# Two blocks of the first batch transposed a second time, in the rounded four-byte type, with the scaled difference added to the residual

## The chip, the cores and the metric

One core of a Trainium2 chip runs the kernel. The metric is the device time of one execution in microseconds (us), the median of several. The engines are named as in the profile: PE (TensorE matmuls), PEld (its weight loads), DVE (VectorE), ACT (ScalarE), POOL (GpSimd) and SP (SyncE, which issues the DMAs here).

## The reference

Attention with normalised queries and keys, then a block that mixes by a Fourier transform and applies a feed-forward network (FFN):

```python
q_n, k_n = rmsnorm(q, g_q), rmsnorm(k, g_k)          # 8 batches, 12 heads, 448 rows, 64 columns
attn = softmax(q_n @ k_n^T / sqrt(64));  x = attn @ v   # as (8, 448, 768)
mixed = real(fft(fft(x, axis=1), axis=2))
u = x + mixed
un = (u - mean(u)) / sqrt(var(u) + 1e-6)
out = u + maximum(un @ w_ch1, 0) @ w_ch2              # 768 -> 3072 -> 768
```

The two weights come as eight-byte doubles, so the kernel also converts them.

## The kernel before

The work goes batch by batch. For a batch, `attention(b)` runs over six pairs of heads: load, normalise (`norm_pair`, "ss" is the sum of squares, "qkn" the normalised q and k), transpose (qk, QT, KD), scores S, softmax (P, transposed as pt into T), value product av, and the result, channels on partitions, in xT. Even and odd sums of xT (eo) feed `spectral(b)`: matmuls y with the transform's matrix give Y, matmuls ab give two banks, whose second is copied to bs, and their sum and difference go into the tile smdf.

The mixed rows fall into four tiles, `token_tile(t, mirror, ...)`: t is 0 or 1 for two halves of the row indices, mirror says whether the rows are the mirrored ones; a tile's number is i4 = 2·mirror + t. For mirror 0 ACT copies the rows, reversed, from xT to xr (the last column by a second small copy where t is 0). PE transposes six blocks of 128 columns with the identity ident, three into each of two banks (x, halves 0 and 1). DVE adds half a tile of smdf to each bank and gets u and its row sums st. SP stores u to DRAM (u_dram), ACT makes un = u − mean. Later `deviation` lets ACT square un into u's place, so this step overwrites u and waits for the store of u; in batch 0 it stands behind all four tiles in the code, but the scheduler may place it earlier. In names, u0_2 is batch 0 and i4 = 2; x0_100 is batch 0, t = 1, mirror 0, half 0.

PE then transposes un into unT (ACT and DVE empty those banks), and `ffn(b)` runs 3456 matmuls h (line L992) and as many o (L1013) over all batches. The mixing and attention of batch b + 1 are woven between the FFN matmuls of batch b.

The weights are converted on the way, in batch 0: `convert` loads a piece of doubles (dbl, line L746, into one of two buffers), ACT takes two passes (mag L749, dbl L750), DVE three (L751, L755, L759), POOL one (L763), ACT makes the rounded part w (L764) and DVE the remainder (L765); SP stores the result (L793) for later batches. Converted pieces lie in streams of three buffers. Line L114 is that of a helper which records every operation; such rows are told apart by their tiles.

The order of each engine's instructions is made by a list scheduler when the program is built, from the code's order and modelled durations; it also chooses buffers. On one engine instructions run in that order. PSUM banks are named by tags; the banks of x come from the tag "either", which alternates between two.

At the start, POOL makes ident (done at about 2.1 us), and PE runs 16 warm-up matmuls with it (L1063) before the first product of the input, qk (L334).

Of the kernel before, what the change touches and what calls it, by code (L numbers as in the profile page):

```python
# [11 lines left out]
F32 = mybir.dt.float32  # L12
F32R = mybir.dt.float32r
# [3 lines left out]
ALU = mybir.AluOpType  # L17
# [73 lines left out]
def spectral_block(ctx, tc, q, k, v, g_q, g_k, w1, w2, d1, d2, out, nb=B):  # L91
    nc = tc.nc
    PSUM = bass.MemoryType.PSUM

    cpool = ctx.enter_context(tc.tile_pool(name="cpool", bufs=1))
    sb = ctx.enter_context(tc.tile_pool(name="sb", bufs=2))
# [23 lines left out]
    V, A, G = Recorded(nc.vector), Recorded(nc.scalar), Recorded(nc.gpsimd)  # L120
# [28 lines left out]
    def bank(tag, name):  # L149
        if tag == "either":  # L150
            tag = ("q", "av")[turn[0] % 2]
            turn[0] += 1
        return ps.tile([128, 512], F32, tag=tag, name=name, bufs=BANKS[tag])
# [3 lines left out]
    def slot(tag, name, dtype=F32):  # L157
        return sb.tile([128, 900], dtype, tag=tag, name=name, bufs=SLOTS[tag])
# [4 lines left out]
    def sub(o, a, b_):  # L163
        V.tensor_tensor(out=o, in0=a, in1=b_, op=ALU.subtract)

    def add(o, a, b_):
        V.tensor_tensor(out=o, in0=a, in1=b_, op=ALU.add)

    def rows_of(n):

        return [slice(a, z) for a, z in ((0, n - n % 16), (n - n % 16, n)) if a < z]
# [5 lines left out]
    G.memset(KL.bitcast(F32), 0.0)  # L177
    ident = cpool.tile([128, 128], F32, name="ident")
    make_identity(nc, ident)
    nhalf = cpool.tile([128, 16], F32, name="nhalf")  # L180
    G.memset(nhalf, -0.5)
    gains = cpool.tile([128, 2], F32, name="gains")
# [29 lines left out]
    X_BANKS = (("either", "either"), ("either", "either"))  # L212
# [388 lines left out]
    def spectral(b, xT, EO, uns):  # L601
        a_, b_, c_ = EO
        Y = {}
        for ri in range(2):
            for st in range(2):
                n = (N1, N2)[st]
                t0 = ri * NT + st * N1
                y = bank(Y_BANKS[b > 0][st], f"y{b}_{ri}_{st}")
                yc = y[:n, :NK].rearrange("t (c i) -> t c i", c=6)
                for par in range(2):  # L610
                    turned = yc[:, 2:5:2] if par == 0 else yc[:, 1:6:4]
                    for i, (o, src, cols) in enumerate((
                        (turned, a_, slice(0, 2 * NI)),
                        (turned, b_, slice(2 * NI, 4 * NI)),
                        (yc[:, 3 * par], c_, slice(4 * NI, 5 * NI)),
                    )):
                        nc.tensor.matmul(  # L617
                            o, src[:, par, t0 : t0 + n], D1[:, ri, par, cols],
                            start=i != 1, stop=i != 0,
                        )  # L620
                Yt = slot("PT", f"Y{b}_{ri}_{st}", F32R)[:n, : 2 * NK].rearrange(
                    "s (i n) -> s i n", i=2
                )
                A.copy(Yt[:, 0], y[:n, : NK])
                sub(Yt[:, 1], y[:n, : NK], Yt[:, 0])
                Y[ri, st] = Yt
                yield 1080

        def token_tile(t, mirror, sm, df):
            i4 = 2 * mirror + t  # L630
            n = LENS[i4]
            place = "h" if b == 0 else "P"
            u = slot("P", f"u{b}_{i4}")[:n, :DM]
            st = sb.tile([N1, 4], F32, tag="st", name=f"st{b}_{i4}", bufs=4)
            if mirror:
                src = xT[:, :, 226 - t : S : 2]
            else:
                xr = slot(place, f"xr{b}_{t}")[:, : NR * n].rearrange(
                    "r (p t) -> r p t", p=NR
                )  # L640
                A.copy(xr[:, :, :N2], xT[:, :, 222 + t :: -2])
                if t == 0:
                    A.copy(xr[:, :, N2:], xT[:, :, 224:225])
                src = xr
            low, high = (df, sm) if mirror else (sm, df)
            for half in range(2):
                xp = bank(X_BANKS[b > 0][half], f"x{b}_{t}{mirror}{half}")
                for i in range(3):
                    nc.tensor.transpose(  # L649
                        xp[:n, i * 128 : (i + 1) * 128], src[:, 3 * half + i], ident  # L650
                    )
                V.scalar_tensor_tensor(
                    out=u[:, half * 384 : half * 384 + 384],
                    in0=xp[:n, :384],
                    scalar=0.0,
                    in1=high[:n, 384:0:-1] if half else low[:n, :384],
                    op0=ALU.add,
                    op1=ALU.add,
                    accum_out=st[:n, half : half + 1],
                )  # L660
            for r in rows_of(n):
                nc.sync.dma_start(u_dram[b % 2, i4, r, :DM], u[r])
            V.tensor_scalar(
                out=st[:n, 2:3], in0=st[:n, 0:1], scalar1=st[:n, 1:2], scalar2=-1.0 / DM,
                op0=ALU.add, op1=ALU.mult,
            )
            un = slot(place, f"un{b}_{i4}")[:n, :DM]
            A.activation(un, u, AF.Identity, bias=st[:n, 2:3])
            uns[i4] = un
            return i4, u, un, st  # L670

        def deviation(i4, u, un, st):
            n = LENS[i4]
            A.activation(u, un, AF.Square, accum_out=st[:n, 3:4])
            rstd = sb.tile([N1, 1], F32, tag="rstd", name=f"rstd{b}_{i4}", bufs=8)
            V.tensor_scalar(
                out=st[:n, 3:4], in0=st[:n, 3:4], scalar1=1.0 / DM, scalar2=EPS,
                op0=ALU.mult, op1=ALU.add,
            )
            G.tensor_tensor(  # L680
                out=rstd[:n], in0=st[:n, 3:4], in1=nhalf[:n, :1], op=ALU.pow
            )
            rstds[b, i4] = rstd

        rest = []
        for t in range(2):
            n = (N1, N2)[t]
            ab = []
            for i in range(2):
                o = bank("S", f"ab{b}_{t}_{i}")[:n, : NK]  # L690
                c = abs(t - i)
                kk = (N1, N2)[c]
                for x_, (a, z) in enumerate(((0, 0), (0, 1), (1, 0))):
                    nc.tensor.matmul(  # L694
                        o, D2[:kk, i, t, a, :n], Y[i, c][:, z], start=x_ == 0, stop=x_ == 2
                    )
                ab.append(o)
            bs = slot("P", f"bs{b}_{t}")[:n, : NK]
            A.copy(bs, ab[1])
            sdt = slot("P", f"smdf{b}_{t}")[:n, : 2 * NK].rearrange(  # L700
                "s (i n) -> s i n", i=2
            )

            def nat(ap):
                return ap.rearrange("t (i c) -> t c i", c=6)

            def half(ap):
                return ap.rearrange("t (c i) -> t c i", c=6)

            add(nat(sdt[:, 0]), half(ab[0]), half(bs))  # L710
            sub(nat(sdt[:, 1]), half(ab[0]), half(bs))
            yield 980
            for mirror in range(2):
                made = token_tile(t, mirror, sdt[:, 0], sdt[:, 1])
                if b:
                    deviation(*made)
                else:
                    rest.append(made)
                yield 620
        for made in rest:  # L720
            deviation(*made)
# [387 lines left out]
```

## Time and profile before

| | us |
|---|---|
| median of three runs | 2168.9 (2167.07 to 2169.48) |
| span of the profiled execution | 2158.8 |
| PE busy | 2085.6 (97%) |
| DVE busy | 1551.6 (72%) |
| ACT busy | 1053.9 (49%) |
| POOL busy | 343.4 (16%) |

The span runs from the first to the last instruction that the profiler records; the run's time lies 10.1 us above it. Batch 0's attention takes the first 140 us, its mixing runs to about 177, and the first h of the FFN is at 177.06. Rows of a timeline give start, duration, engine, line, operation and tiles; in brackets stands how long the engine was idle before and what it waited for.

### The profile page before, as it was taken

The page shows a single profiled execution, that of the slowest core. Times are in us where ns is not written, and L with a number is a line of the kernel's source. Part 1 is how long each engine was busy: PE and PEld are TensorE (multiplying, and loading weights), DVE is VectorE, ACT ScalarE, POOL GpSimd, SP SyncE. Part 2 cuts the span into 40 slices and gives each one's busy share as a digit, 9 for nine tenths or more (in the row PEclk, how much of TensorE's full clock was granted, in tenths as well). Part 3 has the DMA queues.
Part 4 walks back from the last instruction along what each step waited for, and adds up shares of the span by engine and source line. Part 5 has one row for each costly group of instructions (what it writes and reads, how often), then busy time and mean ns, then how long its engine had stood idle before and what let it go on. Part 6 is the DMA issues. An engine that isn't in the chain of part 4 may idle for free.

```text
span 2158.8 us, 31384 instructions
## 1 busy us (share of the span) xinstructions
PE 2085.6 (97%) x11224; PEld 1858.1 (86%) x11224; DVE 1551.6 (72%) x3016; ACT 1053.9 (49%) x2258; POOL 343.4 (16%) x196
## 2 busy tenths in 40 slices
PE   7878999899999999999999999999999999999998
PEld 4557788788999999999999999999999989999998
DVE  7888788877885788758786688857787578754122
ACT  7967776455552555435552455425553355422100
POOL 4323334311110111001110011101110011000000
PEclk8977999999999999999999999999999999999999
DMA  5548877757555855667555666558556674458774
GB/s 172 181 125 272 257 249 255 243 200 214 170 167 182 238 180 168 175 206 225 161 176 177 215 197 176 171 190 239 171 165 188 204 209 142 150 175 251 234 248 150
DMA packets 294976, 424.79 MB, mean 197 GB/s; under 512 B 183283, under 2 KB 221156, under 8 KB 294820
## 3 DMA queue, kind: packets, MB, share of 16 engines
q1 hardware_dynamic: 290386, 420.67, 63.5%
q10 hardware_dynamic: 4434, 2.11, 0.4%
q8 instruction: 89, 1.46, 0.3%
q14 instruction: 67, 0.55, 0.1%
HBM read 362.53 MB, written 65.31 MB: 198 GB/s over the span
## 4 chain that ended last, share of the span: by engine, by line
PE 77%; DMA 3%; DVE 3%; ACT 1%; issue 1%; POOL 0%; DVEq 0%; SPq 0%; POOLq 0%; ACTq 0%
PE h L992 28%; PE o L1013 28%; PE S L382 5%; PE av L492 4%; PE pt L480 4%; DMA dbl<-w 2%; PE y L617 1%; PE qk L334 1%; PE oT L949 1%; PE x L649 1%; PE un L861 1%; PE av L497 1%; PE ab L694 1%; PE rem L437 1%; DMA u_dram<-u 1%
## 5 line engine op out<-in xcount | busy, mean ns | idle before, releaser
L1013 PE MATMUL o<-hs,w 128*128 128x448 f32 x3456 | 793.2, 372 | 2.9 <-DVE rounded L114 0.9
L992 PE MATMUL h<-unT,w 128*128 128x448 f32 x3456 | 784.0, 371 | 1.0 <-DVE hs L114 0.6
L1013 PEld LDWEIGHTS o<-hs,w 128*128 128x128 f32 x3456 | 638.4, 188 | 60.5 <-issue 3.8
L992 PEld LDWEIGHTS h<-unT,w 128*128 128x128 f32 x3456 | 639.8, 189 | 57.5 <-issue 4.1
L114 ACT ACTIVATE P<-S,mn 112x448 f32<-112x448 f32 x384 | 243.9, 637 | 196.9 <-DVE mn L114 188.1
L114 DVE TENSOR_REDUCE mn<-S 112x1 f32<-112x448 f32 x384 | 233.8, 617 | 33.0 <-PE S L382 30.3
L114 ACT ACTIVATE hs<-h 128x448 fp32r<-128x448 f32 x192 | 104.4, 544 | 304.5 <-PE h L992 302.9
L114 DVE SCALAR_TENSOR_TENSOR hs<-h,hs 128x448 fp32r<-128x448 f32 x192 | 119.3, 621 | 149.3 <-ACT hs L114 147.3
L114 DVE TENSOR_TENSOR acc<-o,acc 128x448 f32<-128x448 f32 (+1 forms) x240 | 147.0, 613 | 81.8 <-PE o L1013 79.1
L114 POOL TENSOR_TENSOR qkn<-raw 112x1024 f32<-112x1024 f32 x36 | 69.2, 1924 | 677.4 <-PE qk L334 391.5
L114 POOL TENSOR_TENSOR ss<-ss,nhalf 112x16 f32<-112x16 f32 x48 | 143.6, 2992 | 205.6 <-DVE ss L114 183.6
L382 PE MATMUL S<-KD,QT 128*112 128x448 f32 x384 | 152.8, 400 | 18.5 <-ACT KD L114 15.6
L114 ACT CAST T<-pt 128x448 fp32r<-128x448 f32 x216 | 112.9, 533 | 101.5 <-PE pt L480 97.9
L492 PE MATMUL av<-T,vhl 128*128 128x448 f32 x432 | 154.2, 385 | 0.8 <-DVE T L114 0.8
L114 DVE TENSOR_TENSOR T<-pt,T 128x448 fp32r<-128x448 f32 x216 | 131.7, 617 | 25.7 <-ACT T L114 24.7
L382 PE MATMUL S<-rounded,QT 128*112 128x448 f32 x384 | 143.7, 376 | 0.0
L114 DVE TENSOR_SCALAR P<-P,sm 112x448 f32<-112x448 f32 x288 | 122.7, 465 | 3.9
L480 PE MATMUL pt<-ident,P 112*128 112x112 f32 x864 | 122.1, 258 | 0.0
L480 PEld LDWEIGHTS pt<-ident,P 112*128 112x128 f32 x864 | 102.7, 140 | 15.8
L763 POOL TENSOR_TENSOR mag<-mag,dbl 128x512 uint32<-128x512 uint32 (+1 forms) x46 | 77.6, 1686 | 170.3 <-DVE mag L759 115.2
L114 POOL TENSOR_TENSOR rstd<-st,nhalf 112x1 f32<-112x1 f32 (+2 forms) x32 | 18.2, 570 | 505.7 <-DVE st L114 500.1
L382 PEld LDWEIGHTS S<-KD,QT 128*112 128x112 f32 x384 | 68.5, 179 | 29.4 <-ACT KD L114 18.7
(116 smaller groups left out, 2528.3 us busy)
## 6 DMA issues: line engine op xcount, KB each, us to landing
w<-w SPq DMA_DIRECT2D x192, 768.0 KB, 5.4
w<-w SPq DMA_DIRECT2D x288, 512.0 KB, 4.5
dbl<-w SPq DMA_DIRECT2D x28, 512.0 KB, 5.3
dbl<-w SPq DMA_DIRECT2D x18, 768.0 KB, 5.1
raw<-q SPq DMA_DIRECT2D x96, 112.0 KB, 3.9
raw<-k SPq DMA_DIRECT2D x96, 112.0 KB, 4.0
v<-v SPq DMA_DIRECT2D x96, 96.0 KB, 3.6
u_dram<-u SPq DMA_DIRECT2D x24, 336.0 KB, 3.1
```

The lines of the kernel that those rows point to most:

```text
L114: ins = emit(*args, **kwargs)
L334: nc.tensor.transpose(pt[:, c * C : (c + 1) * C], qk[:, i, c].rearrange("t h d -> t (h d)"), ident[:C, :C],)
L382: ins = nc.tensor.matmul(s_, QT[:, h, cs], K[:, h], start=step == 0, stop=step == 1)
L437: nc.tensor.transpose(rem[:, c * C : (c + 1) * C], Pc[c][:, 384:512], ident[:C, :C])
L480: nc.tensor.transpose(pt[:, c * C : (c + 1) * C], Pc[c][:, 512 * h + j * 128 : 512 * h + (j + 1) * 128], ident[:C, :C],)
L492: nc.tensor.matmul(av[:, :S], lv, T[:, i], start=(j == 0 and i == 0), stop=False)
L497: nc.tensor.matmul(av[:, :S], lv, R[:, h], start=False, stop=True)
L617: nc.tensor.matmul(o, src[:, par, t0 : t0 + n], D1[:, ri, par, cols], start=i != 1, stop=i != 0,)
L649: nc.tensor.transpose(xp[:n, i * 128 : (i + 1) * 128], src[:, 3 * half + i], ident)
L763: behind(nc.gpsimd.tensor_tensor(out=bits, in0=bits, in1=low, op=ALU.add))
L992: pace(nc.tensor.matmul(o, w[:, a, c], unT[c][:, z], start=n == 0, stop=n == 17))
L1013: pace(nc.tensor.matmul(o, w[:, a, f], hs[4 * g + f][:, z], start=n == 0, stop=n == 11))
```

## The change

A second identity, identr, in the rounded four-byte type F32R, is copied from ident by ACT at the start. In batch 0, for the two tiles with mirror 0, SP copies the first three blocks of xr to a tile xq of that type, PE transposes these into a bank with identr, ACT copies the bank to xc, DVE makes xc the difference of the plain transpose and xc, and DVE adds 1e6 times this difference to the half of smdf that the tile's u is made from.

```diff
     ident = cpool.tile([128, 128], F32, name="ident")
     make_identity(nc, ident)
+    identr = cpool.tile([128, 128], F32R, name="identr")
+    A.copy(identr, ident)
...
                 src = xr
+                if b == 0:
+                    xq = sb.tile([128, 384], F32R, tag="xq", name=f"xq{t}", bufs=1)
+                    nc.sync.dma_start(
+                        xq[:, :3*n].bitcast(F32), xr[:, :3].rearrange("r p t -> r (p t)")
+                    )
+                    xqp = bank(X_BANKS[b > 0][1], f"xq{b}_{t}{mirror}")
+                    for i in range(3):
+                        nc.tensor.transpose(
+                            xqp[:n, i * 128 : (i + 1) * 128].bitcast(F32R), xq[:, i*n:i*n+n], identr
+                        )
+                    xc = sb.tile([128, 384], F32, tag="xc", name=f"xc{t}", bufs=1)
+                    A.copy(xc[:n], xqp[:n, :384])
...
                         xp[:n, i * 128 : (i + 1) * 128], src[:, 3 * half + i], ident
                     )
+                if b == 0 and not mirror and not half:
+                    sub(xc[:n], xp[:n, :384], xc[:n])
+                    V.scalar_tensor_tensor(out=low[:n, :384], in0=xc[:n], scalar=1e6, in1=low[:n,:384], op0=ALU.mult, op1=ALU.add)
```

The scheduler's order changes around it. On ACT, from the copy bs of t = 1 to the first unT, before:

```order
L114 COPY bs0_1_1545<-ab0_1_1_1541 112x390
L114 ACTIVATE un0_2_1535<-u0_2_1520,st0_2_1521 111x768
L114 COPY xr0_1_1565<-xT0_295 128x672
L750 ACTIVATE dbl_0_1_1628<-dbl_0_1_1628 128x768
L114 ACTIVATE u0_0_1500,st0_0_1501<-un0_0_1518 113x768
...
L114 ACTIVATE un0_1_1579<-u0_1_1563,st0_1_1564 112x768
...
L114 ACTIVATE un0_3_1595<-u0_3_1581,st0_3_1582 112x768
L114 CAST unT0_0_1685<-un0_0_1680 128x448
```

And now (lines below the change have moved, L749 and L750 are L766 and L767 here):

```order
L114 COPY bs0_1_1557<-ab0_1_1_1553 112x390
L114 ACTIVATE u0_0_1502,st0_0_1503<-un0_0_1530 113x768
L114 ACTIVATE un0_2_1547<-u0_2_1532,st0_2_1533 111x768
L114 COPY xr0_1_1577<-xT0_297 128x672
...
L766 ACTIVATE mag_0_1_1649<-dbl_0_1_1650 128x768
L114 COPY xc1_1585<-xq0_10_1581 112x384
...
L114 ACTIVATE un0_1_1601<-u0_1_1575,st0_1_1576 112x768
...
L114 ACTIVATE un0_3_1617<-u0_3_1603,st0_3_1604 112x768
L781 CAST w1_0_2_1661<-mag_0_2_1662 128x768
L766 ACTIVATE mag_0_4_1677<-dbl_0_4_1678 128x768
L767 ACTIVATE dbl_0_4_1678<-dbl_0_4_1678 128x768
L114 CAST unT0_0_1707<-un0_0_1702 128x448
```

The Square of u0_0 has moved ahead of un0_2 and xr0_1, the copy xc1 is new behind mag_0_1, and the conversion steps of mag_0_4 now stand ahead of the first unT.

On DVE, the first tile's u and the conversion of the piece mag_0_0, before:

```order
L751 TENSOR_SCALAR mag_0_0_1614<-mag_0_0_1614 128x768
L755 TENSOR_SCALAR mag_0_0_1614<-mag_0_0_1614 128x768
L759 SCALAR_TENSOR_TENSOR mag_0_0_1614<-dbl_0_0_1615,mag_0_0_1614 128x768
L114 TENSOR_TENSOR smdf0_0_1497<-ab0_0_0_1487,bs0_0_1495 113x6x65 x2
L114 SCALAR_TENSOR_TENSOR u0_0_1500,st0_0_1501<-x0_000_1505,smdf0_0_1497 113x384
L114 SCALAR_TENSOR_TENSOR u0_0_1500,st0_0_1501<-x0_001_1510,smdf0_0_1497 113x384
```

And now:

```order
L768 TENSOR_SCALAR mag_0_0_1636<-mag_0_0_1636 128x768
L772 TENSOR_SCALAR mag_0_0_1636<-mag_0_0_1636 128x768
L114 TENSOR_TENSOR smdf0_0_1499<-ab0_0_0_1489,bs0_0_1497 113x6x65 x2
L776 SCALAR_TENSOR_TENSOR mag_0_0_1636<-dbl_0_0_1637,mag_0_0_1636 128x768
L114 SCALAR_TENSOR_TENSOR smdf0_0_1499<-xc0_1513,smdf0_0_1499 113x384
L114 SCALAR_TENSOR_TENSOR u0_0_1502,st0_0_1503<-x0_001_1522,smdf0_0_1499 113x384
L114 SCALAR_TENSOR_TENSOR u0_0_1502,st0_0_1503<-x0_000_1515,smdf0_0_1499 113x384
```

The last step of mag_0_0 has moved behind smdf, and the addition of the difference stands between it and u.

Again on DVE, the stretch around u0_1 as it is now (before, u0_1 stood directly behind the second st of tile 0, with mag_0_1 behind u0_3):

```order
L114 TENSOR_SCALAR st0_2_1533<-st0_2_1533 111x1
L768 TENSOR_SCALAR mag_0_1_1649<-mag_0_1_1649 128x768
L114 TENSOR_TENSOR xc1_1585<-x0_100_1587,xc1_1585 112x384
L772 TENSOR_SCALAR mag_0_1_1649<-mag_0_1_1649 128x768
L114 SCALAR_TENSOR_TENSOR smdf0_1_1559<-xc1_1585,smdf0_1_1559 112x384
L768 TENSOR_SCALAR mag_0_2_1662<-mag_0_2_1662 128x768
L114 SCALAR_TENSOR_TENSOR u0_1_1575,st0_1_1576<-x0_101_1594,smdf0_1_1559 112x384
L776 SCALAR_TENSOR_TENSOR mag_0_1_1649<-dbl_0_1_1650,mag_0_1_1649 128x768
L114 SCALAR_TENSOR_TENSOR u0_1_1575,st0_1_1576<-x0_100_1587,smdf0_1_1559 112x384
```

The two conversions' steps have moved ahead of and between the halves of u0_1, with the subtraction and the addition among them. On PE the three rounded transposes stand between the halves x0_000 and x0_001; x0_001 uses the bank of the rounded ones. On SP the copy to xq0 stands ahead of the load dbl_0_0, that to xq1 behind the stores of u0_2 and ahead of the load dbl_0_2, and dbl_0_1 now stands behind the two stores of u0_0. At the start, ACT's table load and the cast to identr stand ahead of the wait for the first input.

## Rows read from the trace of the kernel before

**Rows 1.** The page: busy time of each engine; the chain that ended last.

```profile
PE 2085.6 (97%) x11224; PEld 1858.1 (86%) x11224; DVE 1551.6 (72%) x3016; ACT 1053.9 (49%) x2258; POOL 343.4 (16%) x196
...
PE 77%; DMA 3%; DVE 3%; ACT 1%; issue 1%; POOL 0%; DVEq 0%; SPq 0%; POOLq 0%; ACTq 0%
```

**Rows 2.** Busy time by stretch: PE, PEld, DVE, ACT, POOL, granted clock, DMA share, GB/s.

```profile
20.00:50.00 30.00, 20.90 (x98) 14.25 (x97) 26.64 (x48) 29.61 (x64) 14.12 (x7) 0.84 0.63 197
...
160.00:178.00 18.00, 9.82 (x41) 8.26 (x42) 14.68 (x37) 13.58 (x22) 6.75 (x6) 0.50 0.70 238
```

**Rows 3.** Timeline of the start: start us, us, engine, line, operation, tiles, idle before.

```profile
2.16 9.34 PE L1063 MATMUL warmed<-warm,ident 128*128 128x512 f32 x16 [2.16 <-POOL ident masks.py:199]
...
4.75 1.28 ACT L114 ACT_TABLE_LOAD   x1 [4.75 <-DMA raw<-k]
...
6.05 1.06 ACT L114 ACTIVATE qkn<-raw 112x1024 f32<-112x1024 f32 x1
...
12.51 1.11 PE L334 MATMUL qk<-ident,qkn 112*128 112x112 f32 x8 [1.02 <-DVE qkn L114]
```

**Rows 4.** Timeline of PE where the mixing begins.

```profile
141.63 1.62 PE L649 MATMUL x<-ident,xr 128*113 128x128 f32 x6 [1.01 <-ACT xr L114]
144.82 1.21 PE L617 MATMUL y<-D,eo 128*113 128x130 f32 x4 [1.57 <-DVE eo L114]
```

**Rows 5.** Timeline of ACT from the first tile to unT.

```profile
141.39 0.18 ACT L114 COPY xr<-xT 128x6 f32<-128x6 f32 x1
...
157.57 0.46 ACT L114 COPY bs<-ab 113x390 f32<-113x390 f32 x1
...
165.17 0.79 ACT L114 COPY xr<-xT 128x672 f32<-128x672 f32 x1
...
167.24 0.84 ACT L114 ACTIVATE u<-un 113x768 f32<-113x768 f32 x1
...
171.58 0.93 ACT L114 ACTIVATE un<-u,st 112x768 f32<-112x768 f32 x1
...
175.02 0.92 ACT L114 ACTIVATE un<-u,st 112x768 f32<-112x768 f32 x1
176.47 1.84 ACT L114 CAST unT<-un 128x448 fp32r<-128x448 f32 x4 [0.54 <-PE un L861]
```

**Rows 6.** Timeline of DVE: smdf and u of the tiles, and one conversion later.

```profile
158.08 0.96 DVE L759 SCALAR_TENSOR_TENSOR mag<-dbl,mag 128x768 uint32<-128x768 uint32 x1
158.96 1.55 DVE L114 TENSOR_TENSOR smdf<-ab,bs 113x390 f32<-113x390 f32 x2
160.34 0.56 DVE L114 SCALAR_TENSOR_TENSOR u<-x,smdf 113x384 f32<-113x384 f32 x1
...
169.03 0.56 DVE L114 SCALAR_TENSOR_TENSOR u<-x,smdf 112x384 f32<-112x384 f32 x1 [0.66 <-POOL rstd L114]
...
415.30 0.56 DVE L751 TENSOR_SCALAR mag<-mag 128x768 f32<-128x768 f32 x1 [3.49 <-ACT mag L749]
```

**Rows 7.** DMA issues by tile: count, KB each, median us from issue to landing.

```profile
dbl<-w SPq DMA_DIRECT2D x18, 768.0 KB, 5.1
...
u_dram<-u SPq DMA_DIRECT2D x24, 336.0 KB, 3.1
...
v<-rounded SPq DMA_DIRECT2D x24, 16.0 KB, 2.0
```

**Rows 8.** Timelines of SP's queue and of POOL.

```profile
161.15 0.37 SPq L746 DMA_DIRECT2D dbl<-w  x1
...
174.87 2.03 POOL L763 TENSOR_TENSOR mag<-mag,dbl 128x768 uint32<-128x768 uint32 x1 [3.72 <-ACT mag L749]
```

**Rows 9.** Busy time by stretch, 186 to 426 us: the sum of eight stretches.

```profile
sum 240.00, PE 231.12 PEld 191.60 DVE 196.44 ACT 163.73 POOL 91.81; mean PE 28.89 PEld 23.95 DVE 24.56 ACT 20.47 POOL 11.48
```

**Rows 10.** Waits of PE, 178 to 500 us: total, times, longest, in us.

```profile
PE y L617 <- DVE eo L114: 4.2, 1, 4.2
```

**Rows 11.** The chain that ended last: start us, us, what.

```profile
406.94 7.35 DMA dbl<-w
```

## The prediction

> **What bounds the kernel now.** The page's first part and its chain come first [rows 1]: PE is busy 2085.6 us of a span of 2158.8 us (97%), and PE has 77% of the chain that ended last. So the change is worth what it does to the few places where PE waits. It touches two of them. The table of stretches [rows 2] shows the larger: PE is busy 9.82 of the 18 us from 160 to 178, at a granted clock of 0.50, while no engine is full (DVE 14.68, ACT 13.58). There the first batch's mixing hands over to its FFN, and a chain of single steps on DVE, ACT, SP and PE rules. The other is the first 12 us [rows 3]. In batch 0's FFN, from 186 to 426, PE is busy 231.12 of 240 us [rows 9], so 8.9 us are all that is idle there. Next the rows of PE, ACT and DVE in the handover [rows 4 to 6] give the steps' durations, and the landings of DMAs [rows 7] what a copy costs. From batch 1 on the changed kernel has its old order nearly throughout; what is decided before about 480 us is simply carried.
>
> The added work as such is small. Six transposes are 1.62 us of PE by the six that stand there now [rows 4]; two ACT copies of 384 columns cost 0.46 each by the bs row [rows 5]; four DVE operations of 0.56 each by the u row make 2.2 [rows 6]. What counts is the chain they lengthen, and the neighbours the scheduler changed.
>
> **Part 1, the start.** PE's warm-up, which reads ident, starts at 2.16; ACT's table load starts at 4.75, when the first k is there, and the Square at 6.05 [rows 3]. In the new order the table load and the cast to identr stand ahead of the wait for the input, so both run in ACT's dead time, and the Square can start when the data is there: up to 1.28 earlier, and so can ss, qkn and the first qk. But PE's warm-up matmuls run from 2.16 to 11.50, and PE waits only 1.02 more before qk at 12.51. So the gain is at most 1.0, and at least 0. I take −1.0, because ACT, which the next stretch hangs on, is busy 29.61 of 30 us from 20 to 50 [rows 2] and keeps what it is given. A page differs on the size, though not on the sum: the Trainium skill, ScalarE: Activation LUTs, What ACT_TABLE_LOAD costs, gives 1283 ns for the load and 1380 ns for a drain. The row has 1.28, and the Square 0.02 after it, so no drain shows here; with one the gain would be 2.66, and the warm-up would cap it at 1.0 as well.
>
> **Part 2, the tile t=0.** The last column of xr is written at 141.57 [rows 5]. From there: the copy to xq, which SP issues and PE now waits for. The nearest rows are v<-rounded, also from on-chip memory to on-chip memory, 16 KB in 2.0, and u_dram<-u, 336 KB in 3.1 [rows 7]; xq has 174 KB, and I take 2.6 (bounds 2.0 and 3.1). Landed 144.2; three transposes 0.8; the copy to xc 0.46, which the second half's transposes wait for, because x0_001 takes xq's bank; these 0.8. So y starts at 146.3 against 144.82 [rows 4], +1.5. On the size of the copy a page speaks: the Trainium skill, DMA: Bandwidth & Descriptors, Latency and other measured facts, says that the access to HBM is the dominant part of a DMA's fixed 2 us; this copy touches no HBM. The 2.0 row touches none either, so the row gives little sign of such a saving; by the page the copy would lie at 2.0 or under, and the sum would be about 1.2 less over the two copies.
>
> Of these 1.5 little reaches smdf: it started at 158.96 because DVE was still in the last step of mag_0_0 (158.08 for 0.96) [rows 6], and this step has been moved behind smdf. smdf stays at 159.0; then come the moved step (0.9) and the new addition (0.55). u0_0, at 160.34 before, is +1.4, and un0_0 behind it.
>
> **Part 3, the tile t=1.** Here the order changes for the worse. The Square of u0_0 now stands on ACT ahead of un0_2 and of the copy xr0_1. It overwrites u0_0, so it waits for the two stores of u0_0: end of u 162.7, plus 3.1 [rows 7], 165.8. Square 1.0 (0.84 and a read), 166.9; un0_2 0.84, 167.7; xr0_1 0.79, 168.5, against 165.96 (165.17 and 0.79) [rows 5]: +2.5. Then xq1 lands at 171.1 and is transposed at 171.9. ACT gets to its copy xc1 only behind dbl_0_1 (SP issues it behind the two u0_0 stores, at 0.4 each [rows 8], at 163.6; 5.1 to landing [rows 7], 168.7), two casts, a Square and mag_0_1: five passes of some 0.84 by the Square's row, 172.9, and 173.4 with the copy. On DVE u0_1 stands behind the subtraction, a shift, the new addition and the first step of mag_0_2. Its load is issued behind xq1, at 169.0; with 5.1 to landing and 0.9 on ACT it is there at 175.0, and 0.5 on DVE follow. So u0_1 starts at 175.5, not at 175.0 behind xc1 (173.4, and 1.6 of DVE), against 169.03 [rows 6]: +6.5.
>
> **Part 4, the last two tiles and unT.** Between u0_1 and un0_1 DVE has two halves of u, a mag step of 0.96, another of 0.55, half of u0_3 and st: 3.2, so un0_1 at 178.7, against 171.58 [rows 5] +7.1. un0_3 follows a Square that again waits for a store, and ends at 182.5 against 175.94, +6.6. PE's transposes of un are ready then, but ACT now has mag_0_4 and dbl_0_4 ahead of unT0_0: their load gets its buffer when POOL has done mag_0_1 (DVE at 177.0, POOL 2.03 [rows 8]), at 179.0, lands at 184.1, and two passes of 0.84 take 1.7. unT0_0 at 185.8 against 176.47 [rows 5], +9.3. The FFN's first matmul needs unT0_0; the later columns of unT hang on un0_3 too and not on that load alone, so they come back towards its +6.6. Between 6.6 and 9.3 I take **+8** for the start of the FFN. The low granted clock in this stretch [rows 2] is there in both, and only its end moves.
>
> **Part 5, what batch 0 gives back.** PE is idle 8.9 us from 186 to 426, and then waits 4.2 for eo ahead of y [rows 10]: 13.1 in all could swallow the delay, where what PE waited for does not itself wait for PE. The weight conversions (SP load, ACT, DVE, POOL) don't, until their three buffers are full; attention of batch 1 does, since its S and pt stand between the h. What speaks for giving back is DVE's idle 3.49 for a conversion at 415.30 [rows 6], in front of the eo that y waits for: there DVE waits for ACT and ACT for a load of 7.35 [rows 11], not for PE. I take 3.5; bounds 0 and all. The stretch is also put into another order, which I can't price.
>
> **Sum.** −1.0 + 8.0 − 3.5 = +3.5 of the span of 2158.8. The median, 2168.9, is 10.1 more than the span of the profiled execution; I add the difference to the median: **2172.4 us**. A measurement of this kernel tells about 0.2% from no change, 4.3 us: 2164.6 to 2173.2.
>
> **The rivals.**
> A, the forecast: late FFN, partly given back: +1 to +7, 2170 to 2176. Chance 0.55.
> B, all of it hidden: conversions and loads go on while PE waits, and PE catches up in its 13.1 idle us. Then −1 + 8 − 8, 2168, within −2 and +1 with the short copy. For it: the chain of work there runs over the loads and not over PE, as these two rows show; against: PE's idle is in small pieces, behind attention's own results. 0.20.
> C, faster: the idle of batch 0 goes for good, because while PE stands the conversions and batch 1's attention run ahead by as much, and no later wait comes back. −1 + 8 − 13.1 = −6.1, 2163. It decides faster by over 0.2% from 11.3 swallowed. Against it: conversions can only be three buffers ahead. 0.08.
> D, nothing given back or more added: the new order of batch 0 brings waits of its own, or ACT's waits for loads are longer than 5.1 because the DMA engines are already at 0.70 there [rows 2]. +7 to +12, 2176 to 2181, about 2178. 0.17.
> That the edit does nothing is no rival for time: its instructions stand in the order; whether the rounded transpose differs from the plain one is a value, multiplied and added either way.
>
> **How the numbers follow.** D and A's upper part lie over 2173.2: 0.17 + 0.23 = 0.40 slower; C's larger part is faster, 0.06; same 0.54. The range leaves out C and the far ends of D and B: 2167 to 2179. The likeliest case by itself has 2170 to 2176.
>
> **What would show it.** Right: the Square of qkn at about 4.8 and qk at 11.5; y at 146; u0_1 at 175 and unT0_0 at 185 with ACT waiting for dbl_0_4; less than 8.9 of PE idle in the FFN. Wrong: unT0_0 under 180 (the load or the stores land sooner, or DVE is ahead), a wait of over 5 for xq, or new waits of PE between 200 and 480.

## The result

The changed kernel takes 2177.0 us (median of five runs, 2173.8 to 2183.7) against 2168.9 for the kernel before: a ratio of 1.0054, with a 95% interval from 1.0040 to 1.0069. That is slower by more than 0.2%, and more than the +3.5 us of the forecast. A second comparison gave 1.0038 (1.0024 to 1.0053). Both say slower, by 8 to 12 us.

Runs of the kernel before spread from 2159 to 2172 us, and its profile shown ahead belongs to one of its quickest. The profiled execution of the changed kernel took 2179.3 us with a span of 2177.3, so about 2 us lie outside a span, and the 10.1 of the prediction were mostly the distance between a quick run and the median. The two spans therefore differ by more (18.5) than the kernels do, and a second profile of the kernel before (`b_again`, below, span 2164.7) is used as its partner from here on.

The page of the changed kernel: its span, the busy times, the chain that ended last.

```profile
span 2177.3 us, 31352 instructions
...
PE 2092.2 (96%) x11230; PEld 1860.8 (85%) x11230; DVE 1554.1 (71%) x3020; ACT 1056.0 (48%) x2261; POOL 340.6 (16%) x196
...
PE 78%; DMA 9%; DVE 5%; ACT 5%; issue 2%; POOL 1%; SPq 0%; DVEq 0%; POOLq 0%; ACTq 0%
```

Against [rows 1]: PE's work is nearly the same (2092.2 us busy against 2085.6). The shares of the two chains can't be set side by side: this one is followed back to the start, that of before only to 313.85 us, so its shares come to 85% of the span.

The start, in the timeline (start us, us, engine, line, operation, tiles, idle before); it answers to [rows 3]:

```profile
0.73 1.28 ACT L114 ACT_TABLE_LOAD   x1 [0.73 <-PEq L1109]
...
5.15 1.06 ACT L114 ACTIVATE qkn<-raw 112x1024 f32<-112x1024 f32 x1 [2.72 <-DMA raw<-k]
...
11.63 1.10 PE L336 MATMUL qk<-ident,qkn 112*128 112x112 f32 x8
```

The table load has moved into ACT's dead time, and qk starts 0.88 earlier. The handover to the FFN, timelines of PE, then ACT, then DVE, POOL and PE again; they answer to [rows 4 to 6]:

```profile
144.02 0.83 PE L654 MATMUL xq<-identr,xq 128*113 128x128 f32 x3 [1.14 <-DMA xq<-xr]
145.42 0.98 PE L663 MATMUL x<-ident,xr 128*113 128x128 f32 x3 [0.57 <-ACT xc L114]
146.19 1.07 PE L619 MATMUL y<-D,eo 128*113 128x130 f32 x4
...
171.45 0.56 PE L654 MATMUL xq<-identr,xq 128*112 128x128 f32 x3 [2.22 <-DMA xq<-xr]
```

```profile
165.84 0.84 ACT L114 ACTIVATE u<-un 113x768 f32<-113x768 f32 x1 [1.64 <-DMA u_dram<-u]
...
167.50 0.79 ACT L114 COPY xr<-xT 128x672 f32<-128x672 f32 x1
170.06 0.88 ACT L767 ACTIVATE dbl<-dbl 128x768 uint32<-128x768 uint32 x1 [1.77 <-DMA dbl<-w]
...
173.70 0.45 ACT L114 COPY xc<-xq 112x384 f32<-112x384 f32 x1
...
180.66 0.94 ACT L114 ACTIVATE un<-u,st 112x768 f32<-112x768 f32 x1 [4.87 <-issue]
...
183.89 0.82 ACT L781 CAST w<-mag 128x768 fp32r<-128x768 f32 x1
184.62 0.89 ACT L766 ACTIVATE mag<-dbl 128x768 f32<-128x768 f32 x1
185.41 0.90 ACT L767 ACTIVATE dbl<-dbl 128x768 uint32<-128x768 uint32 x1
186.21 1.81 ACT L114 CAST unT<-un 128x448 fp32r<-128x448 f32 x4
```

```profile
175.24 0.55 DVE L114 SCALAR_TENSOR_TENSOR smdf<-xc,smdf 112x384 f32<-112x384 f32 x1
175.71 0.55 DVE L768 TENSOR_SCALAR mag<-mag 128x768 f32<-128x768 f32 x1
176.17 0.55 DVE L114 SCALAR_TENSOR_TENSOR u<-x,smdf 112x384 f32<-112x384 f32 x1
...
178.00 1.98 DVE L772 TENSOR_SCALAR mag<-mag 128x768 uint32<-128x768 uint32 x1
```

```profile
177.74 1.83 POOL L780 TENSOR_TENSOR mag<-mag,dbl 128x768 uint32<-128x768 uint32 x1 [3.81 <-DVE mag L776]
```

```profile
186.77 0.74 PE L1009 MATMUL h<-unT,w 128*128 128x448 f32 x1 [1.72 <-ACT unT L114]
```

The steps of the prediction stand here in its order: the Square waits for the store, then xr, the load, xc, u0_1 at 176.2, un0_1 at 180.7, unT at 186.2. Two of its waits do not: DVE has no idle time from 173.83 to u0_1, so the load of mag_0_2, whose step stands ahead of it, had come by then; and ACT has none between 180.66 and unT, so it did not wait for dbl_0_4 either. The first h, at 177.06 in the profile ahead and 178.69 in `b_again`, is at 186.77. Busy times of the two stretches around it (PE, PEld, DVE, ACT, POOL, granted clock, DMA share, GB/s):

```profile
160.00:178.00 18.00, 7.03 (x27) 5.16 (x27) 12.56 (x33) 9.51 (x15) 4.54 (x5) 0.50 0.62 208
178.00:200.00 22.00, 15.49 (x75) 13.25 (x76) 19.30 (x36) 16.96 (x30) 10.11 (x7) 0.69 0.87 298
```

In the first, PE has 7.03 us of work where it had 9.82 [rows 2]. And the waits of PE from 195 to 520 (total, times, longest):

```profile
PE av L458 <- ACT T L114: 7.3, 6, 2.3
PE un L878 <- ACT un L114: 4.8, 1, 4.8
PE y L619 <- DVE eo L114: 3.5, 1, 3.5
```

The wait for eo [rows 10] has hardly shrunk, so little was given back there, and the waits for T have grown: `b_again` has 2.1 us of them in three. One of them, on PE and, just ahead of it, on ACT:

```profile
265.55 2.31 PE L458 MATMUL av<-T,v 128*128 128x448 f32 x4 [1.97 <-ACT T L114]
```

```profile
263.75 0.89 ACT L767 ACTIVATE dbl<-dbl 128x768 uint32<-128x768 uint32 x1 [2.24 <-DMA dbl<-w]
264.54 0.53 ACT L114 ACTIVATE hs<-h 128x448 fp32r<-128x448 f32 x1
264.97 0.96 ACT L114 COPY T<-pt 128x448 f32<-128x448 f32 x2
```

ACT stands in front of a conversion step whose load has not landed, with T queued behind it, and PE waits for T. It is a wait of the new order, not of the new work: `before_neworder` (below), which has the one without the other, has it too (2.01 us at 264.1).

### The profile page after: what moved, and what is told of

Same layout as the page of the kernel before. It is cut to its first block, busy times and chain, and to the rows that moved or that the text cites. A ratio compares the mean times of both kernels' runs of the same rounds, so it can differ in the third digit from the quotient of the medians.

```text
span 2177.3 us, 31352 instructions
## 1 busy us (share of the span) xinstructions
PE 2092.2 (96%) x11230; PEld 1860.8 (85%) x11230; DVE 1554.1 (71%) x3020; ACT 1056.0 (48%) x2261; POOL 340.6 (16%) x196
## 4 chain that ended last, share of the span: by engine, by line
PE 78%; DMA 9%; DVE 5%; ACT 5%; issue 2%; POOL 1%; SPq 0%; DVEq 0%; POOLq 0%; ACTq 0%
PE h L1009 28%; PE o L1030 27%; PE S L384 6%; DMA dbl<-w 5%; PE av L494 4%; PE pt L482 4%; DMA u_dram<-u 2%; PE y L619 2%; PE qk L336 1%; PE av L458 1%; POOL mag L780 1%; PE oT L966 1%; ACT P L114 1%; DMA w<-w 1%; PE rem L439 1%
## 5 line engine op out<-in xcount | busy, mean ns | idle before, releaser
L780 POOL TENSOR_TENSOR mag<-mag,dbl 128x512 uint32<-128x512 uint32 (+1 forms) x46 | 77.1, 1675 | 176.8 <-DVE mag L776 137.4
L384 PEld LDWEIGHTS S<-KD,QT 128*112 128x112 f32 x384 | 69.0, 181 | 31.3 <-ACT KD L114 19.7
```

Of the source, the lines that this page charges most:

```text
L384: ins = nc.tensor.matmul(s_, QT[:, h, cs], K[:, h], start=step == 0, stop=step == 1)
L780: behind(nc.gpsimd.tensor_tensor(out=bits, in0=bits, in1=low, op=ALU.add))
```

## The experiments

Two theories and a rival. **Handover**: what costs is the FFN's late start. **Order**: what costs is the other order of batch 0's FFN. **Work**: the copies and added steps cost it, however ordered. The scheduler mixes all three, so most kernels here hold every engine to a given order from the first instruction into batch 1's FFN, by dependencies that only fix the order of issue (PINNED lists, for each engine, the numbers of its instructions in the order to hold; the cuts further down give a list in words):

```diff
+PINNED = {
...
+    for numbers in PINNED.values():
+        row = [f"I-{n}" for n in numbers.split()]
+        for one, two in zip(row, row[1:]):
+            tc.add_manual_dep(
+                nc.get_inst_by_name(two), one,
+                mybir.DependencyInfo(mybir.DependencyClass.NoSync, mybir.DependencyReason.DATA),
+                reason="issue order",
+            )
```

"Old" is the order of the kernel before, "new" that of the changed one; the cut between handover and FFN is the last unT on each engine (on POOL the last rstd of batch 0, on SP the last store of u). The times below are ratios to the kernel before, run on the same chip; 0.001 is 2.2 us. The expectations quote differences of means, which lie within 1 us of these. That holding an order costs nothing in itself was not measured alone; `before_warm` below, held to the old order, comes to 0.9995.

| kernel | handover | FFN | added work | ratio (95%) | first h | first h to second FFN |
|---|---|---|---|---|---|---|
| b_again | old | old | no | 1 | 178.7 | 296.8 |
| before_newhandover | new | old | no | 1.0019 (1.0010, 1.0029) | 185.7 | 292.1 |
| before_newffn | old | new | no | 1.0021 (1.0010, 1.0032) | 178.0 | 301.7 |
| before_neworder | new | new | no | 1.0030 (1.0017, 1.0043) | 185.9 | 297.4 |
| after_oldorder | old | old | yes | 1.0007 (0.9994, 1.0019) | 181.6 | 298.4 |
| after_oldffn | new | old | yes | 1.0031 (1.0019, 1.0042) | 186.1 | 295.5 |
| after_oldhandover | old | new | yes | 1.0039 (1.0026, 1.0053) | 179.8 | 304.2 |
| after_again | new | new | yes | 1.0038 (1.0024, 1.0053) | 187.7 | 301.0 |

The last column is the time from the first h of batch 0 to the first of batch 1, in us, with 1392 or 1393 recorded matmuls in each. Its source for three of them and for the first profile of the changed kernel, as stretches with busy times (b_again, before_newhandover, before_newffn, after):

```profile
178.69:475.44 296.75, 279.86 (x1392) 236.19 (x1393) 235.83 (x398) 191.39 (x373) 103.38 (x63) 0.97 0.76 249
```

```profile
185.72:477.77 292.05, 276.60 (x1393) 233.40 (x1393) 231.51 (x392) 189.16 (x369) 100.34 (x61) 0.98 0.75 248
```

```profile
177.95:479.64 301.69, 280.82 (x1393) 236.26 (x1393) 239.68 (x398) 192.48 (x373) 102.16 (x64) 0.96 0.75 245
```

```profile
186.77:488.61 301.84, 281.48 (x1392) 235.68 (x1393) 233.06 (x392) 189.42 (x369) 99.93 (x61) 0.96 0.74 240
```

**b_again**: the kernel before, unchanged, for a second profile.

> The kernel before, profiled a second time. Its five times lie between 2161.9 and 2169.5, and its first profile has a span of 2158.8, which belongs to the lowest. Handover theory and order theory alike: a span of about 2159 to 2167, with the first h at 177 again. If a span near 2166 shows, the places where it differs from the first are what varies from run to run, and have to be kept out of the comparison.

One time, 2166.5, span 2164.7, the first h at 178.69. It is 1.6 later there than in the first profile and 6.0 later at the end; it serves as the partner of the profiles below.

**identr_only**: the cast to identr, nothing else; every other row keeps its place.

```diff
     make_identity(nc, ident)
+    identr = cpool.tile([128, 128], F32R, name="identr")
+    A.copy(identr, ident)
```

> Only the cast to identr at the start; every engine's order is else that of before. Term 1 of the prediction: ACT's table load at about 0.7, the first qk about 0.9 earlier, and all of it carried: -0.9 us, between -1.5 and 0. If the start is not on the path: 0.

1.0003 (0.9988 to 1.0018). The first qk is at 11.49:

```profile
11.49 1.11 PE L336 MATMUL qk<-ident,qkn 112*128 112x112 f32 x8 [0.49 <-DVE qkn L114]
```

So the start is 1.0 earlier, as predicted, but at the end a gain of 1.0 can't be told from none within this interval. Whether it is carried stays open. The trace also shows how far single profiles differ: with the order of before, its stretch from the first h to the second FFN is 4.1 shorter than that of `b_again`, and the profile ahead has 295.90. So a few us in this stretch tell little without the ratio beside them.

```profile
177.85:470.50 292.65, 276.12 (x1393) 233.84 (x1393) 235.78 (x398) 191.81 (x373) 103.51 (x63) 0.97 0.77 253
```

**after_oldorder**: the changed kernel, old order throughout.

```diff
+PINNED = the order of before, the new instructions free between
```

> The changed kernel, all its work, with every engine held to the order of before (order-only dependencies up to batch 1); the new instructions stand between. Handover theory (what is late at the start of the FFN is kept): u0_1 waits for xq1 and xc1, some 4 us later, first h at about 180 to 181 and a time of +2 to +4 us over before. Order theory (the reordering costs, the work nearly nothing): 0 to +3. Work theory (the copies over SP and the extra steps cost it all, however they are ordered): +10 to +12.

1.0007 (0.9994 to 1.0019), first h at 181.57. The work theory falls for this kernel: all the added work costs about 1.5 us when the order stays, not 8 to 12.

**before_neworder**: nothing added, new order throughout.

```diff
+PINNED = the order of the changed kernel, without its new instructions
```

> The work of before, with every engine held to the order of the changed kernel. Order theory: nearly the whole loss, +8 to +12 us, with PE waiting 5 us or more for T in the FFN as in the changed kernel. Handover theory: the Square's wait for the stores and the conversions ahead of u0_1 and unT are there, the copies to xq are not, so the first h at 183 to 185 and +6 to +8. Work theory: 0 to +2.

1.0030 (1.0017 to 1.0043): +6.5 us without one added instruction, the first h at 185.91. Most of the loss is the order. The time fits the handover theory better and the waits for T fit the order theory, so the two were cut apart.

**after_again**, the changed kernel beside the next three.

```diff
 (no edit to the changed kernel)
```

> The changed kernel once more, beside the same runs of before as the three that follow. If order and work add up from the two held kernels (+7.0 for the order, +1.6 for the work): +8 to +9. If the two make each other worse: +10 to +13 as in the first comparison. First h at 185 to 187.

1.0038, +8.2 us: what the order (+6.5) and the work (+1.5) give together.

**before_newhandover** and **before_newffn**: each half of the new order alone.

```diff
+PINNED = new up to the last unT, old from there      (before_newhandover)
+PINNED = old up to the last unT, new from there      (before_newffn)
```

> The work of before; new order only up to the last unT, the old order in the FFN and batch 1's attention. Handover theory: first h at about 186, and +6 to +8 us, as in the kernel with the new order throughout. FFN-order theory (the reordered FFN makes the loss): 0 to +2, since the late start is made up.

> The work of before; old order up to the last unT, the new order after it. Handover theory: first h at about 178, 0 within 2 us. FFN-order theory: +5 to +8 us, with PE waiting 2 us each three times for T as in the changed kernel.

1.0019 and 1.0021: each theory foresaw one of them at nothing, and both cost some 4 us. With the new handover alone the first h is 7.0 later than in `b_again`, and the stretch behind it 4.7 shorter (296.75 to 292.05), which is no more than `identr_only` differs without a late start. The ratio says it better: +4.1 at the end (2.2 to 6.3) of 7.0, so some 3 us were given back. PE's wait for eo, 4.2 to 4.3 us in `before`, `b_again` and `identr_only`, is 1.8 here. With the new FFN order alone the first h is not late at all, the stretch is 4.9 longer, and PE waits for T (from 195 to 520, in before_newffn and then in `b_again`):

```profile
PE av L466 <- ACT T L124: 5.2, 6, 2.3
```

```profile
PE av L456 <- ACT T L114: 2.1, 3, 1.4
```

In the eight kernels of the table these waits come to 5.2 to 8.4 us where the FFN order is new and to 0.5 to 2.1 where it is old.

**after_oldhandover** and **after_oldffn**: the same cut in the changed kernel.

```diff
+PINNED = old up to the last unT, its own from there  (after_oldhandover)
+PINNED = its own up to the last unT, old from there  (after_oldffn)
```

> The changed kernel with all its work; old order up to the last unT, its own order after it. Handover theory: first h at 181 to 182 and +1 to +3, as with the old order throughout. FFN-order theory: +7 to +9.

> The changed kernel with all its work; its own order up to the last unT, the old order after it. Measured so far against before: new handover order +3.8, new FFN order +4.4, both +7.1, the work in the old order +1.7, all of the change +9.1. If the FFN order is a cost of its own that a late start does not hide: +4 to +6, first h at 187. If only the late start counts: +8 to +9.

1.0039 and 1.0031. With the first, the expectation of the handover theory (+1 to +3) was missed and that of the FFN order (+7 to +9) met: with the new FFN order, a first h 7 us earlier brought nothing. With the second, +6.7 us was above what I had put (+4 to +6), within the interval. Averaged over the four pairs of the table that differ in one column alone, the new handover costs 2.8 us, the new FFN order 3.8 and the work 2.4. They don't simply add: a late first h costs 4.1 and 5.2 with the old FFN order, 2.0 and −0.2 with the new one. The mixtures also have waits of their own: PE waits 3.1 us and more for KD near 195 where old handover meets new FFN, which neither whole order has, so each figure is good to a microsecond or two.

**before_newffn_a**: only the first part of the new FFN order. It was meant to reach about 310 us; in the trace PE and ACT leave the new order for the old near 275 us and DVE near 285.

```diff
+PINNED = old, new from the last unT to about 280 us, old from there
```

> The work of before; new order only in the first half of batch 0's FFN (to about 310 us), the old order before and after it. One-place theory (the wait of PE for KD at 194, 3.3 us with a stretch of half clock behind it, is most of the loss): +3 to +4.5. Many-places theory (waits for T spread over the whole FFN): +1.5 to +2.5.

1.0003 (0.9994 to 1.0012). Both expectations missed: this part costs nothing that can be measured, although the wait for KD is in it (2.01 us at 194.6). What the new FFN order costs lies behind some 280 us or needs both parts; the second part alone was not tried. The waits for T go with the loss: 0.5 us here, and of the 5.2 in before_newffn 4.1 at 337 and 391. In the traces the kernels also part there in the pace of the conversions, POOL's step for each piece. Six pieces in a row, the first and the last of them, in before_newffn and then in before_newffn_a:

```profile
296.75 1.29 POOL L773 TENSOR_TENSOR mag<-mag,dbl 128x512 uint32<-128x512 uint32 x1 [1.24 <-ACT T L124]
...
336.32 1.79 POOL L773 TENSOR_TENSOR mag<-mag,dbl 128x512 uint32<-128x512 uint32 x1 [1.70 <-DVE mag L769]
```

```profile
298.88 1.31 POOL L773 TENSOR_TENSOR mag<-mag,dbl 128x512 uint32<-128x512 uint32 x1 [3.10 <-DVE sums L124]
...
332.65 2.35 POOL L773 TENSOR_TENSOR mag<-mag,dbl 128x512 uint32<-128x512 uint32 x1 [2.18 <-ACT P L124]
```

39.6 us for these in the new order, 33.8 in the old one. In all the kernels up to here the last of these POOL steps and the start of the second FFN move together, 25 to 27 us apart: 449.9 and 475.4 in b_again, 453.3 and 479.6 in before_newffn, 461.9 and 488.6 in the changed kernel.

**before_warm**: matmuls without use in PE's gaps of the handover, old order.

```diff
+KEPT = 34
...
+    kept = bank("ffn", "kept")
+    for _ in range(KEPT):
+        nc.tensor.matmul(kept[:, :128], ident, ident, start=True, stop=True)
+PINNED = old, 10, 8, 12 and 4 of these in the four gaps from 157 to 176
```

> Before, in its own order, with 34 matmuls of ident by ident (128 columns, results unread) in the four gaps of PE between 157 and 176. If the half clock at the start of the FFN comes from PE's idle time in the handover: granted clock over 0.8 from 178 on, the first eight h in 2 us in place of 3.3, and 1 to 4 us less in all. If the clock does not follow them: 0 within 1.5, or +1 where they overrun a gap.

0.9995 (0.9986 to 1.0005), the same. The stretches of this kernel:

```profile
160.00:178.00 18.00, 13.38 (x96) 12.02 (x95) 14.68 (x37) 13.65 (x22) 6.42 (x6) 0.88 0.69 238
178.00:200.00 22.00, 21.47 (x103) 18.15 (x102) 19.72 (x33) 16.99 (x31) 9.92 (x6) 0.86 0.84 283
```

The granted clock followed in the first stretch (0.88, it was 0.50 [rows 2]); but PE still waited 3.09 us ahead of un0_1, and the first h ran at the half clock as before (0.74 us, at a granted clock of 0.50 from 176.9 to 178.5). What filling that gap too would give stays open.

**t0_only**: the change on the tile t = 0 alone, the scheduler free.

```diff
-                if b == 0:
+                if b == 0 and t == 0:
...
-                if b == 0 and not mirror and not half:
+                if b == 0 and t == 0 and not mirror and not half:
```

> The change on tile t = 0 alone; half of the added work, and the scheduler makes an order of its own again (the Square of u0_0 ahead of un0_2 as in the changed kernel, other places in the FFN). Work theory: +0.8. Order theory: not half of the change's +9.1, but what its own order gives: the first h at 182 to 186, and +2 to +9.

1.0025 (1.0014 to 1.0036), +5.4 us for half of the work, with the first h at 178.14, no later than before. The expected late first h did not come; the loss did, in the stretch behind it (302.2 us). Its order is again another one, and PE's waits for T come to 6.2 us (195 to 520, 2.1 in `b_again`), with one of 2.9 for xT and one of 2.2 for hs beside them.

**Third buffers.** That POOL's steps move with the end could make the conversion loop the cause or a follower. The next kernels hold the order and give the loop a third buffer, for the loaded doubles (tag X, which the eo tiles share) and for the words made from them (M).

```diff
-    SLOTS = {"P": 8, "PT": 6, "M": 2, "unT": 6, "h": 6}
+    SLOTS = {"P": 8, "PT": 6, "M": 3, "unT": 6, "h": 6}
...
-        return sb.tile([128, 1800], dtype, tag="X", name=name, bufs=2)
+        return sb.tile([128, 1800], dtype, tag="X", name=name, bufs=3)
```

`before_3buf_old` is before with its own order, `before_x3_old` and `before_m3_old` have one of the two lines; `after_3buf_own` and `after_3buf_old` are the changed kernel in its own and in the old order, `after_3buf` leaves the scheduler free.

> Before, in its own order, with three buffers in place of two for the loaded doubles and for the words made from them, so that a load no longer waits for POOL's last step two pieces back. Conversion theory (the two-buffer loop of load, ACT, DVE, POOL is what batch 0's FFN keeps step with; its 60th POOL step at 447 to 450 now): that step 3 us or more earlier, and 2 to 7 us less in all. PE theory (PE, 94 to 95 per cent busy there, sets the pace): ACT's waits for loads go, but the time is the same within 1.5.

> Before, own order, a third buffer for the loaded doubles alone. Conversion theory with the load's wait as its cause: most of the -12.9, between -13 and -8. If the wait is for the other buffer (the words made from them): -3 to 0.

> Before, own order, a third buffer for the words made from the doubles alone. Conversion theory with the load's wait as its cause: -3 to 0. If the wait is for this buffer (ACT's mag pass waits until DVE's last step two pieces back): -13 to -8.

> The changed kernel in its own order with the same third buffers. Conversion theory: its 60th POOL step comes down from 462 to 455 or less, and the loss against before shrinks from +9.1 to between 0 and +5. PE theory: still +8 to +10.

> The changed kernel with the third buffers and the scheduler free to make a new order. Conversion theory: as the one before, 0 to +5, or less where the scheduler also uses the slack. Order theory alone: anything between 0 and +9, as its new order happens to fall.

> The changed kernel, all its work, in the order of before, with the third buffers. Conversion theory: what the order cost is gone and the loop has its slack: about -12 (before with third buffers: -12.9) plus 1.7 for the work in this order, so -13 to -9, faster than both kernels. If work and buffers interfere: -8 to 0.

| kernel | ratio (95%) | first h | first h to second FFN |
|---|---|---|---|
| before_3buf_old | 0.9939 (0.9927, 0.9951) | 174.6 | 286.5 |
| before_x3_old | 0.9945 (0.9931, 0.9959) | 173.9 | 286.5 |
| before_m3_old | 0.9989 (0.9980, 0.9999) | 177.7 | 294.3 |
| after_3buf_own | 1.0013 (1.0004, 1.0022) | 186.7 | 291.6 |
| after_3buf | 1.0005 (0.9996, 1.0014) | 188.1 | 289.5 |
| after_3buf_old | 0.9988 (0.9979, 0.9998) | 180.7 | 288.1 |

The loop is a cause and not a follower: with no instruction moved, a third buffer of the tag X makes the kernel before 12 us quicker (`before_x3_old`, 2151.6 us), which beats both kernels and is more than the 2 to 7 us I expected of both buffers; the buffer of the words alone gives 2.4. How much of the 12 us is the loads' and how much that of the eo tiles, which share the tag, was not separated. Its stretch from the first h to the second FFN, and its last POOL step in the timeline, at 434.6 against 449.9:

```profile
173.93:460.43 286.50, 274.37 (x1392) 231.97 (x1393) 238.73 (x398) 191.56 (x373) 104.05 (x64) 0.98 0.80 259
```

```profile
434.56 1.53 POOL L773 TENSOR_TENSOR mag<-mag,dbl 128x512 uint32<-128x512 uint32 x1 [1.70 <-DVE mag L769]
```

ACT's waits for loads, from 186 to 450, fall from 48.3 us (24.3 and 24.0 in `b_again`) to 31.3 (and PE's wait for eo from 4.3 to 1.2):

```profile
ACT mag L759 <- DMA dbl<-w: 17.2, 10, 4.2
ACT dbl L760 <- DMA dbl<-w: 14.1, 7, 4.6
```

But my expectation that the change would then cost less was half wrong. Against the kernel before as it is, the loss shrank from 8.2 to 2.8 us, as I had put it. Against the kernel before with the same buffers it grew: `after_3buf_old` is 0.0049 (some 10 us) above `before_3buf_old`, and `after_3buf_own` another 0.0025. The first h is 6.1 and 12.1 later than in `before_3buf_old`, the second FFN starts 7.7 and 17.1 later. My reading is that with two buffers the loop held the kernel before up as well and hid part of the handover's delay behind itself. That is argued and not shown: 10 us at the end are more than the 6.1 at the first h. What the runs show is where the loss grew. The added work in the old order costs some 10 us with three buffers, where it cost 1.5 with two; the new order on top of the work costs 5.4 (`after_3buf_own` over `after_3buf_old`), where it cost 6.7 (`after_again` over `after_oldorder`). The expected −13 to −9 for `after_3buf_old` was missed, with −2.6.

## Why the prediction was wrong

The 2177.0 us lie inside the stated 2167 to 2179, but where rival D put them and not in the likeliest case, which was 2170 to 2176; the +3.5 came out as +8.2 and +11.7. Term by term:

**The start** (−1.0): qk at 11.63 and 11.49, predicted 11.5, the Square at 5.15 and not 4.8, since ACT waited for k until then, and until 4.75 in the profile ahead. At the end `identr_only` shows 0 ± 3 us, so the term is neither shown nor excluded.

**The handover** (+8): right in the time of nearly every step, not in every cause. y 146.2 (predicted 146.3), the Square of u0_0 165.8 (165.8), xr done 168.3 (168.5), xc1 at 173.7, done 174.2 (173.4), u0_1 176.2 (175.5), un0_1 180.7 (178.7), unT0_0 186.2 (185.8). For u0_1 the forecast had the load of mag_0_2 as what comes last, and for unT0_0 that of mag_0_4. In the trace neither was waited for: u0_1 stood behind xc1 and DVE's steps, and unT0_0 behind un0_1, 2.0 late, and a row of passes on ACT without a gap. That the times still fit within 0.7 and 0.4 us is in part luck. The first copy to xq took from 141.87, its issue, to 144.02, when PE starts on it, the second from 168.32 to 171.45: 2.1 and 3.1, with the 2.6 that I took between them. The page of the Trainium skill that I weighed there (DMA: Bandwidth & Descriptors, Latency and other measured facts) pointed to less; these copies, without HBM, still took 2.1 and 3.1, so the saving does not show here. The FFN began 8.1 after that of `b_again`.

**What batch 0 gives back** (−3.5 of 8): 2.9 in `before_newhandover`, which starts its FFN 7.0 late and ends +4.1; its shorter wait for eo is the place the forecast named. With the added work it is less: `after_oldffn` starts 7.4 late and ends +6.7, 0.7 given back. Each is good to 2 or 3 us, so the two can't be told apart.

**The step that failed** is the last sentence of that part: "The stretch is also put into another order, which I can't price", and so it stood in the sum at nothing. `before_newffn`, that order alone and no late start, costs 4.5 us (1.0010 to 1.0032); over the four pairs of the table the new FFN order costs 3.8, from 6.9 with the work in the old handover to 1.5 in the changed kernel itself. With it a late or early first h makes little difference (2.0 and −0.2 us between the pairs), so the two prices do not add. It was no unknown without bounds: the lists that hold PE to the two orders (in `before_x3_old` and `before_newffn`) differ at 600 of their 3000 positions, in a stretch where PE, the conversion loop and batch 1's attention keep each other waiting by turns [rows 9 to 11]. That a new order there need not be neutral `t0_only` shows again: half the change drew another order and lost 5.4. Two draws give no average.

**The added work**, taken at nothing beyond the handover, costs 1.5 us in the old order (1.0007, 0.9994 to 1.0019) and 2.4 on average over four pairs, which fits its 3 us at the first h, partly given back.

Put together: handover and giving back +4.1, FFN order +4.5, together 6.5 and not 8.6, work +1.5, the start 0: +8.0 against 8.2 and 11.7 measured. Counted the other way, all that the prediction priced comes to +6.7 and not +3.5 (`after_oldffn`), and the new FFN order adds the last 1.5. Rival D had this (new waits of its own in the FFN, +7 to +12), at 0.17; the waits for T in the trace are of the kind it needed. In rival C the late start was to let the conversions run ahead; what did that here is a third buffer, in the kernel before.

## What to carry to other kernels

Where a scheduler orders the instructions, an edit's price has two parts, its work and the new order; hold the old order by order-only dependencies, and each is measured by itself. Here the added work cost 1.5 us and the reordering 6.5. The two prices belong to the kernel they were measured in: with three buffers the same work cost some 10 us. And where PE is 94% busy, a two-buffer loop beside it may still set the pace: give it a third buffer with the order held, and see whether the time moves, before reading a late start as hidden or carried.

## What was unexpected of the hardware

DVE's shift of a 128x768 piece takes 0.55 us where POOL is idle. In the changed kernel one took 1.98, from 178.00 to 179.98 (the row above), while POOL's step ran from 177.74 to 179.57. That is most of the 2.0 by which un0_1 came later than predicted. Rows of about 2 us are in `b_again` too: the same shift at 176.8 (2.07), and the step ahead of it, for 128x512 pieces, at 329.9 and 337.3 (1.99 and 2.13), each under a step of POOL. The Trainium skill (SBUF — State Buffer, section "SBUF: two separate sides") says that DVE, for some kinds of its operations, and GpSimd share a pair of ports that one of them holds for a whole instruction while the other is blocked. The rows agree, in that the shift ends 0.4 after POOL's step; but not every shift that overlaps POOL is slow here: of 15 such in the changed kernel 11 took their usual time, 0.4 us for 512 columns and 0.55 for 768.
